# One time line for all tiles, one activation table set, and one-hot columns kept by stage

## The chip, the core and the metric

The kernel runs on one core of a Trainium2 chip. The core has five engines that run their own instruction streams in order and wait for each other at semaphores: TensorE (PE, matmuls; PEld is its weight load), VectorE (DVE), ScalarE (ACT), GpSimd (POOL) and SyncE (SP, which here only issues loads). The metric is the device time of one execution in microseconds. The kernel before takes 1128.44 us (median of 3 runs, 1127.2 to 1128.48).

## What is computed

x has 2 batches of 16000 rows with 512 channels, in bf16. The reference, cut to what matters:

```python
z = sum(xp[:, i:i+T, :] * dw_enc[i] for i in range(3))   # depthwise filter over time
z = silu(z)
res, q = z, 0
for s in range(4):                                       # four codebooks of 8 rows
    cb = codebooks[s]
    d2 = sum(res * res) - 2.0 * res @ cb.T + sum(cb * cb)
    idx = d2.argmin(-1)
    q, res = q + cb[idx], res - cb[idx]
y = sum(qp[:, i:i+T, :] * dw_dec[i] for i in range(3))   # second depthwise filter
```

## The kernel before, in words

The rows are cut into 18 tiles of 1792 rows (128 partitions by G = 14 groups), which overlap by two rows. A tile passes through five steps:

- **load**: 14 transposing DMAs on SP (L213) bring x, with the channels on the partitions, into one of two buffers XT (XT0 and XT1, in the trace XT_149 and XT_150). Two POOL copies (L214, L215) fill the halo columns. A load into a buffer waits until the last reader of the tile before in it has run.
- **front**, for each of the four 128-channel parts: three multiplications by a filter tap (the taps, L222) and two additions (L225, L226) on DVE; then SiLU without a division, Exp on ACT (L227), plus one on DVE (L232), Ln and Exp on ACT (L234, L235), and the product on DVE (the gate, L240) into one of three buffers ZB.
- **select**: PE makes the products of each row with itself and with the codebooks (L252, L255), DVE reduces them (L273, L274), and then decides stage 0, 1 and 2 in a chain of small operations (L296 to L311); between two stages a correction by the codebooks' products goes over PE (L318 to L341). A decision ends in a one-hot block OH (L311), which POOL copies (L312) into the tile's array OHA. Then PE transposes OHA in seven windows (L350), and DVE copies them to OHW (L351).
- **resid**: 24 updates subtract the chosen codebook rows from ZB. PE does the matmuls with OHW (L362, L363) into one of three PSUM buffers; three of four updates are written back by ACT (L367), the fourth by DVE (L369). The score of the last codebook (L283, L284), its decision and a second pass of the windows follow.
- **back**: seven decodes, two or three matmuls each (L380 to L384), copied by ACT into Y (L385), and the stores, issued by POOL (L408).

ACT holds one set of function tables at a time; the built program has a table load wherever the next function is not in the set that is held. Exp and Ln come from different sets in the kernel before.

The order in which the code records its steps is made at the end: iteration n takes the steps of front for tile n, select for n-1, resid for n-2 and back for n-3, spreads each list evenly over the iteration, and sorts. A scheduler of the framework then makes the engines' streams from these steps with its own costs; it moves instructions, and it fixes their order on each engine.

Of the kernel before, what the change touches and what calls it, by code (L numbers as in the profile page):

```python
# [17 lines left out]
def kernel(  # L18
# [41 lines left out]

    IDENT = const.tile([P, P], BF16, name="IDENT")
# [12 lines left out]
    WDBC = const.tile([P, K, D], BF16, name="WDBC")  # L74
    CB4 = const.tile([P, D], BF16, name="CB4")
    cbf = codebooks.flatten_outer_dims()
    wd_rows = bass.AP(tensor=dw_dec.tensor, offset=dw_dec.offset, ap=[[0, P], [D, K], [1, D]])
    with nc.allow_non_contiguous_dma(reason="small weights"):
        for k in range(K):
            nc.scalar.dma_start(out=WENC_b[:, :, k], in_=dw_enc[k].rearrange("(i p) -> p i", p=P))  # L80
        for j in range(4):
            nc.scalar.dma_start(out=CB4[NC * j:NC * (j + 1), :], in_=cbf)
        nc.scalar.dma_start(out=WDBC, in_=wd_rows)
# [6 lines left out]
    for i in range(KT):  # L90
        pt = psS.tile([P, 512], F32, name="pt", tag="pss")
        ptb = pt.bitcast(BF16)[:, 0:NC]
        nc.tensor.transpose(ptb, CB4[0:NC, i * P:(i + 1) * P], IDENT[0:NC, 0:NC])
        nc.vector.tensor_copy(CBT[:, i, :], ptb)
        nc.vector.tensor_scalar(out=CBM2[:, i, :], in0=ptb, scalar1=-2.0, scalar2=None, op0=ALU.mult)
# [65 lines left out]


    WDEC = []
    for v, taps in enumerate(((0, 1, 2, None), (None, 0, 1, 2), (None, None, 0, None), (None, 2, None, None))):
        w = const.tile([P, D], BF16, name=f"WDEC{v}")
        nc.gpsimd.memset(w, 0.0)
        for j, tap in enumerate(taps):
            if tap is not None:
                nc.vector.tensor_tensor(out=w[NC * j:NC * (j + 1), :], in0=CB4[NC * j:NC * (j + 1), :],
                                        in1=WDBC[NC * j:NC * (j + 1), tap, :], op=ALU.mult)  # L170
# [3 lines left out]
    for s in range(3):  # L174
        SM = const.tile([P, 1], F32, name=f"SM{s}")
        nc.vector.tensor_reduce(out=SM, in_=IDENT.rearrange("p (j s c) -> p j s c", s=Nq, c=C)[:, :, s, :], axis=AX.XY, op=ALU.add)
        nc.vector.tensor_scalar(out=SM, in0=SM, scalar1=-1.0, scalar2=None, op0=ALU.mult)
        for u in range(2):
            w = const.tile([P, D], BF16, name=f"CBN{s}_{u}")
            nc.gpsimd.memset(w, 0.0)  # L180
            j = 1 + u
            nc.vector.tensor_scalar(out=w[NC * j:NC * (j + 1), :], in0=CB4[NC * j:NC * (j + 1), :],
                                    scalar1=SM[NC * j:NC * (j + 1), :], scalar2=None, op0=ALU.mult)
# [4 lines left out]
    OHA = [const.tile([P, G + 2, NC], BF16, name=f"OHA{b}") for b in range(NOH)]  # L188
# [97 lines left out]
    def decide(st, s):  # L286
# [23 lines left out]
        OH = small.tile([P, G, C], BF16, name="OH")  # L310
        nc.vector.tensor_tensor(out=OH, in0=KY, in1=M.to_broadcast([P, G, C]), op=ALU.is_equal)  # L311
        nc.gpsimd.tensor_copy(OHA[st["n"] % NOH][:, 1:G + 1, cs], OH)  # L312
# [32 lines left out]
    def windows(st):  # L345
# [3 lines left out]
        for k in range(GH):  # L349
            nc.tensor.transpose(pwb[:, k * P:(k + 1) * P], A[:, 2 * k:2 * k + 4, :].rearrange("p g c -> p (g c)"), IDENT)  # L350
        nc.vector.tensor_copy(W[:, :, PADC:PADC + P], pwb[:, 0:GH * P].rearrange("p (k c) -> p k c", c=P))  # L351
# [68 lines left out]
    def select(st):  # L420
# [6 lines left out]
        yield lambda: windows(st)  # L427

    def resid(st):
# [9 lines left out]
        yield lambda: windows(st)  # L439
# [4 lines left out]

    NT = len(tiles)
    load(tiles[0])
    for n in range(NT + 3):
        if n + 1 < NT:
            load(tiles[n + 1])
        steps = []  # L450
        for off, gen in ((0, front), (1, select), (2, resid), (3, back)):
            if 0 <= n - off < NT:
                w = list(gen(tiles[n - off]))
                steps += [((j + 0.5) / len(w), off, f) for j, f in enumerate(w)]
        for _, _, f in sorted(steps, key=lambda t: t[:2]):
            f()
# [30 lines left out]
```

## Time and profile before

| | |
|---|---|
| runs | 1128.48, 1127.2, 1128.44 us |
| profiled execution | 1130.45 us, span of its instructions 1128.6 us |
| mean granted TensorE clock | 0.843 |
| ACT busy | 919.7 us (81%) |
| DVE busy | 768.0 us (68%) |
| PE busy | 667.1 us (59%) |
| POOL busy | 103.2 us (9%) |
| table loads on ACT | 137, 1283 ns each |
| loads of a tile | 18, each of 14 DMAs, 18.2 to 23.2 us to issue |

The share of an engine is its busy time over the span. A row of a timeline gives start and duration in microseconds; a row of a group gives the busy time, the mean of one in nanoseconds, and the idle time of the engine just before it. "A <- B" names what ended a wait. PEclk is the clock that TensorE was granted, as a share of its full speed. Names carry a buffer number (ZB_122, P_3209); P is the scratch of one channel part in front.

### The profile page before, as it was taken

What the parts mean: (1) busy time and instruction counts of PE and PEld (TensorE: products, weight loads), DVE (VectorE), ACT (ScalarE), POOL (GpSimd) and SP (SyncE); (2) the same over time, 40 slices, a digit from 0 to 9 for tenths busy, and PEclk for the clock granted to TensorE, in tenths of its full rate; (3) what the DMA queues carried; (4) which work ended last, traced back from release to release, by engine and by line L of the source; (5) the groups of instructions that cost most, each with busy time, mean ns of one, the idle gap of its engine ahead of it and who ended that gap; (6) DMA issues with size and microseconds to landing.
All of it is one profiled execution on the core that took longest, in us unless ns stands there. A gap on an engine that the chain in (4) does not pass through costs nothing.

```text
span 1128.6 us, 12123 instructions
## 1 busy us (share of the span) xinstructions
PE 667.1 (59%) x4459; PEld 372.7 (33%) x4459; DVE 768.0 (68%) x1520; ACT 919.7 (81%) x803; POOL 103.2 (9%) x219
## 2 busy tenths in 40 slices
PE   0035577473664828474756647575648364759983
PEld 0023244232342414232333324242424232335542
DVE  7897787777566575858666666868675759456631
ACT  0796999999968798887979797989897897956672
POOL 4100101100010100001010100000100100011001
PEclk9987898797886969687887979798969696979996
DMA  5222302314032040504131221414130602020113
GB/s 112 63 63 43 66 9 58 102 29 112 19 77 54 22 109 1 129 1 106 26 89 43 75 57 55 73 50 82 45 86 2 130 1 65 1 66 9 58 65 127
DMA packets 142907, 67.13 MB, mean 59 GB/s; under 512 B 139852, under 2 KB 140460, under 8 KB 140588
## 3 DMA queue, kind: packets, MB, share of 16 engines
q1 hardware_dynamic: 137088, 33.06, 15.1%
q0 software_dynamic: 3840, 32.77, 9.3%
q10 hardware_dynamic: 1920, 0.53, 0.2%
q8 instruction: 35, 0.57, 0.2%
q14 instruction: 24, 0.20, 0.1%
HBM read 0.53 MB, written 32.77 MB: 30 GB/s over the span
## 4 chain that ended last, share of the span: by engine, by line
ACT 45%; SPq 17%; DVE 14%; PE 14%; issue 5%; DMA 3%; POOL 1%; ACTq 0%; POOLq 0%; DVEq 0%
SPq L213 17%; ACT ZB_124 L367 5%; ACT ZB_122 L367 5%; ACT ZB_123 L367 5%; ACT Y L385 5%; ACT LN L234 5%; ACT L235 5%; PE pgr L255 4%; ACT L234 4%; PE pu L363 3%; PE pu L362 3%; DMA XT_150<-in_x_dram 1%; DMA XT_149<-in_x_dram 1%; DVE rr L273 1%; PE pgr L252 1%
## 5 line engine op out<-in xcount | busy, mean ns | idle before, releaser
L385 ACT CAST Y<-py 128x1024 bf16<-128x1024 f32 x126 | 128.1, 1023 | 75.4 <-PE py L384 57.6
L367 ACT CAST ZB_122<-pu 128x896 bf16<-128x896 f32 x108 | 94.0, 907 | 23.3 <-PE pu L363 22.5
L362 PEld LDWEIGHTS <-IDENT 128*128 128x128 bf16 x648 | 69.1, 107 | 124.8 <-DVE S L274 42.2
L362 PE MATMUL pu<-ZB_122,IDENT 128*128 128x512 bf16 (+1 forms) x216 | 85.2, 394 | 29.5 <-DVE S L274 14.8
L367 ACT CAST ZB_123<-pu 128x896 bf16<-128x896 f32 x108 | 93.8, 909 | 10.5 <-PE pu L363 9.6
L362 PE MATMUL pu<-ZB_123,IDENT 128*128 128x512 bf16 x216 | 83.8, 388 | 29.6 <-DVE S L274 12.1
L367 ACT CAST ZB_124<-pu 128x896 bf16<-128x896 f32 x108 | 93.6, 911 | 6.2 <-PE pu L363 5.5
L362 PE MATMUL pu<-ZB_124,IDENT 128*128 128x512 bf16 x216 | 82.9, 384 | 18.7 <-DVE S L274 7.2
L234 ACT ACT_TABLE_LOAD x68 | 87.2, 1283 | 1.2
L255 PE MATMUL pgr<-ZB_122 128*128 128x152 bf16 (+1 forms) x672 | 58.6, 242 | 41.8 <-DVE ZB_122 L240 41.8
L252 PE MATMUL pgr<-MSK,IDENT 128*128 128x456 bf16 (+3 forms) x180 | 64.6, 359 | 21.4 <-ACT Y L385 9.7
L369 DVE TENSOR_TENSOR ZB_124<-ZB_124,pu 128x896 bf16<-128x896 bf16 x36 | 39.1, 1086 | 50.4 <-PE pu L363 50.4
L369 DVE TENSOR_TENSOR ZB_122<-ZB_122,pu 128x896 bf16<-128x896 bf16 x36 | 39.1, 1086 | 48.9 <-PE pu L363 48.9
L255 PEld LDWEIGHTS <-ZB_122 128*128 128x128 bf16 x672 | 52.0, 106 | 56.8 <-DVE ZB_122 L240 43.8
L235 ACT ACT_TABLE_LOAD x54 | 69.3, 1283 | 1.0
L369 DVE TENSOR_TENSOR ZB_123<-ZB_123,pu 128x896 bf16<-128x896 bf16 x36 | 39.1, 1086 | 37.0 <-PE pu L363 37.0
L408 POOL DMA_DIRECT2D out_dram<-Y x66 | 40.2, 613 | 243.5 <-ACT Y L385 243.5
L255 PE MATMUL pgr<-ZB_123 128*128 128x152 bf16 (+1 forms) x672 | 57.4, 238 | 5.1 <-DVE ZB_123 L240 4.9
L255 PEld LDWEIGHTS <-ZB_123 128*128 128x128 bf16 x672 | 50.8, 104 | 24.3 <-issue 12.8
L273 DVE TENSOR_REDUCE rr<-pgr 128x6 f32<-128x768 f32 (+1 forms) x54 | 41.8, 775 | 19.7 <-PE pgr L255 19.3
L255 PE MATMUL pgr<-ZB_124 128*128 128x152 bf16 (+1 forms) x672 | 53.1, 228 | 0.8 <-DVE ZB_124 L240 0.4
L380 PE MATMUL py<-WDEC_211,OHW_259 128*128 128x512 bf16 x35 | 15.7, 449 | 60.8 <-DVE OHW_259 L351 52.5
(1268 smaller groups left out, 1853.7 us busy)
## 6 DMA issues: line engine op xcount, KB each, us to landing
out_dram<-Y POOLq DMA_DIRECT2D x18, 1568.0 KB, 8.4
out_dram<-Y POOLq DMA_DIRECT2D x14, 196.0 KB, 8.1
XT_149<-in_x_dram SPq DMA_TRANSPOSE x126, 2.8
XT_150<-in_x_dram SPq DMA_TRANSPOSE x126, 2.8
out_dram<-Y POOLq DMA_DIRECT2D x30, 12.0 KB, 2.0
out_dram<-Y POOLq DMA_DIRECT2D x2, 210.0 KB, 8.1
WDBC<-in_dw_dec_dram ACTq DMA_DIRECT2D x1, 384.0 KB, 4.4
out_dram<-Y POOLq DMA_DIRECT2D x2, 126.0 KB, 7.8
```

The source lines that it names most:

```text
L213: nc.sync.dma_start_transpose(out=X[:, :, g + 1, :], in_=src[g])
L234: nc.scalar.activation(LN, pk[1], ACT.Ln)
L235: nc.scalar.activation(pk[1], LN, ACT.Exp, scale=-1.0)
L252: nc.tensor.matmul(o, lhsT=IDENT, rhs=MSK[:, 0:nb, c0:c1], start=True, stop=False)
L255: nc.tensor.matmul(o[:, u * w:(u + 1) * w], lhsT=Z[:, i, b0 + u, N3:N3 + P], rhs=Z[:, i, b0 + u, c0:c1], start=False, stop=(u == nb - 1 an ...
L273: nc.vector.tensor_reduce(out=grp(st["rr"], g0, g1)[:, :, :, 0], in_=v[:, :, :, N3:N3 + P], axis=AX.X, op=ALU.max)
L362: nc.tensor.matmul(o, lhsT=IDENT, rhs=zg[:, k0:k0 + nk, :], start=True, stop=False)
L363: nc.tensor.matmul(o, lhsT=CBN[s, u][:, i * P:(i + 1) * P], rhs=W[:, k0:k0 + nk, PADC:PADC + P], start=not on_act, stop=True)
L367: nc.scalar.copy(zg, v)
L369: nc.vector.tensor_tensor(out=zg, in0=zg, in1=v, op=ALU.add)
L385: nc.scalar.copy(Y[:, 2 * k:2 * k + 2, :].rearrange("p g d -> p (g d)"), py)
L408: nc.gpsimd.dma_start(out=view[p0:p1, lo:hi, :], in_=Y[p0:p1, lo:hi, :])
```

## The change

The change has four parts.

1. Before anything else one table set is asked for that has both Exp and Ln.
2. The steps of all tiles go on one time line. Tile n is loaded at n-1; front takes n to n+1, select n+1.05 to n+1.6, resid n+1.6 to n+2.6, back n+2.6 to n+3.4. All steps are sorted by these times once, instead of iteration by iteration.
3. OHA has the stage ahead of the group, so that a decision writes its one-hot block there itself and POOL's copy goes. A window is then 32 columns of one stage; the transposes are made per stage, 21 after the third decision and 7 after the fourth, where there were 7 and 7, and the two copies to OHW take 96 and 32 partitions, where both took 128.
4. The constants follow the new layout: CB4 is loaded by 16 DMAs of 8 rows and CB1 by one, in place of four of 32 rows, and WDEC and CBN are made with masks JM.

```diff
+    nc.scalar.preload_act_table_set("natural_log_exp_and_others")
...
-        for j in range(4):
-            nc.scalar.dma_start(out=CB4[NC * j:NC * (j + 1), :], in_=cbf)
+        nc.scalar.dma_start(out=CB1, in_=codebooks.flatten_outer_dims())
+        for s in range(Nq):
+            for j in range(4):
+                nc.scalar.dma_start(out=CB4[NC * s + C * j:NC * s + C * (j + 1), :], in_=codebooks[s])
         nc.scalar.dma_start(out=WDBC, in_=wd_rows)
...
-    OHA = [const.tile([P, G + 2, NC], BF16, name=f"OHA{b}") for b in range(NOH)]
+    OHA = [const.tile([P, Nq, G + 2, C], BF16, name=f"OHA{b}") for b in range(NOH)]
...
-        OH = small.tile([P, G, C], BF16, name="OH")
+        OH = OHA[st["n"] % NOH][:, s, 1:G + 1, :]
         nc.vector.tensor_tensor(out=OH, in0=KY, in1=M.to_broadcast([P, G, C]), op=ALU.is_equal)
-        nc.gpsimd.tensor_copy(OHA[st["n"] % NOH][:, 1:G + 1, cs], OH)
...
-    def windows(st):
+    def windows(st, s0, s1):
...
         for k in range(GH):
-            nc.tensor.transpose(pwb[:, k * P:(k + 1) * P], A[:, 2 * k:2 * k + 4, :].rearrange("p g c -> p (g c)"), IDENT)
-        nc.vector.tensor_copy(W[:, :, PADC:PADC + P], pwb[:, 0:GH * P].rearrange("p (k c) -> p k c", c=P))
+            for s in range(s0, s1):
+                nc.tensor.transpose(pwb[NC * s:NC * (s + 1), k * P:(k + 1) * P],
+                                    A[:, s, 2 * k:2 * k + 4, :].rearrange("p g c -> p (g c)"), IDENT)
+        r = slice(NC * s0, NC * s1)
+        nc.vector.tensor_copy(W[r, :, PADC:PADC + P], pwb[r, 0:GH * P].rearrange("p (k c) -> p k c", c=P))
...
-        yield lambda: windows(st)
+        yield lambda: windows(st, 0, 3)
...
-    load(tiles[0])
-    for n in range(NT + 3):
-        if n + 1 < NT:
-            load(tiles[n + 1])
-        steps = []
-        for off, gen in ((0, front), (1, select), (2, resid), (3, back)):
-            if 0 <= n - off < NT:
-                w = list(gen(tiles[n - off]))
-                steps += [((j + 0.5) / len(w), off, f) for j, f in enumerate(w)]
-        for _, _, f in sorted(steps, key=lambda t: t[:2]):
-            f()
+    order = []
+    for n, st in enumerate(tiles):
+        order.append((n - 1.0, 0, lambda st=st: load(st)))
+        for off, dur, gen in ((0.0, 1.0, front), (1.05, 0.55, select), (1.6, 1.0, resid), (2.6, 0.8, back)):
+            w = list(gen(st))
+            order += [(n + off + dur * (j + 0.5) / len(w), off, f) for j, f in enumerate(w)]
+    for _, _, f in sorted(order, key=lambda t: t[:2]):
+        f()
```

How this moves instructions, at three places of the steady part. A tap is a TENSOR_SCALAR whose input is XT0 or XT1; before, its line is L222, in the changed kernel L237.

On DVE before, the last two taps of a tile in XT1 are these (P0_3207 and P1_3209):

```order
L304 TENSOR_TENSOR V_2934<-PR3_2843,rr3_2844 128x112
L222 TENSOR_SCALAR P0_3207<-XT1_150,WENC_102 128x1792
L307 TENSOR_TENSOR KEY1_263<-V_2934,CCB_170 128x112
L222 TENSOR_SCALAR P1_3209<-XT1_150,WENC_102 128x1792
L309 TENSOR_REDUCE M_2937<-KEY1_263 128x14
L225 TENSOR_TENSOR P0_3207<-P0_3207,P1_3209 128x1792
```

The next tile in XT1 is first read 29 rows after P1_3209, by P2_3934:

```order
L226 TENSOR_TENSOR P0_3594<-P0_3594,P2_3598 128x1792
L369 TENSOR_TENSOR ZB2_124<-ZB2_124,pu_3032 128x7x128
L222 TENSOR_SCALAR P2_3689<-XT0_149,WENC_102 128x1792
L222 TENSOR_SCALAR P2_3934<-XT1_150,WENC_102 128x1792
L222 TENSOR_SCALAR P2_3996<-XT1_150,WENC_102 128x1792
L232 TENSOR_SCALAR P1_3596<-P1_3596 128x1792
```

So before, 29 of the 80 rows that a tile has on DVE lie between the two; for tiles 3 and 4 it is 69 and 48. On DVE now, the last taps in XT1 are P0_3442 and P1_3444:

```order
L237 TENSOR_SCALAR P0_3442<-XT1_165,WENC_117 128x1792
L316 TENSOR_TENSOR PR_3260<-S_3137,CCF_184 128x112
L237 TENSOR_SCALAR P1_3444<-XT1_165,WENC_117 128x1792
L319 TENSOR_TENSOR V_3262<-PR_3260,TR_3258 128x112
L386 TENSOR_TENSOR ZB2_139<-ZB2_139,pu_3268 128x7x128
L322 TENSOR_TENSOR KEY0_288<-V_3262,CCB_185 128x112
```

The next tile in XT1 is first read by P2_4094:

```order
L241 TENSOR_TENSOR P0_3756<-P0_3756,P2_3760 128x1792
L237 TENSOR_SCALAR P2_3930<-XT0_164,WENC_117 128x1792
L237 TENSOR_SCALAR P2_4094<-XT1_165,WENC_117 128x1792
L247 TENSOR_SCALAR P1_3664<-P1_3664 128x1792
L237 TENSOR_SCALAR P2_4150<-XT1_165,WENC_117 128x1792
L288 TENSOR_REDUCE rr_3622<-pgr_3623 128x6
```

Now 66 rows lie between them, and so for every tile from the third on.

On ACT before, the last update of one tile (ZB1) and the first of the next (ZB2) are almost neighbours, and Exp and Ln with their table loads follow:

```order
L385 CAST Y_2542<-py_2916 128x1024
L367 CAST ZB2_124<-pu_2968 128x7x128
L367 CAST ZB2_124<-pu_2983 128x7x128
L227 ACTIVATE P1_3209<-P0_3207 128x1792
L234 ACT_TABLE_LOAD
L234 ACTIVATE LN_3300<-P1_3209 128x1792
L235 ACT_TABLE_LOAD
L235 ACTIVATE P1_3209<-LN_3300 128x1792
L227 ACTIVATE P1_3454<-P0_3452 128x1792
```

On ACT now, five Exp and Ln stand between the last update cast of ZB1 and the first of ZB2, without a load:

```order
L384 CAST ZB1_138<-pu_2835 128x7x128
L242 ACTIVATE P1_2960<-P0_2958 128x1792
L249 ACTIVATE LN_3012<-P1_2790 128x1792
L250 ACTIVATE P1_2790<-LN_3012 128x1792
L249 ACTIVATE LN_3055<-P1_2960 128x1792
L250 ACTIVATE P1_2960<-LN_3055 128x1792
L384 CAST ZB2_139<-pu_3005 128x7x128
```

The whole ACT stream has one table load now, at its start, where there were 137.

More of the change, by code (lines that the diff above doesn't have):

```diff
@@ L75 @@
     CB4 = const.tile([P, D], BF16, name="CB4")
-    cbf = codebooks.flatten_outer_dims()
+    CB1 = const.tile([NC, D], BF16, name="CB1")
     wd_rows = bass.AP(tensor=dw_dec.tensor, offset=dw_dec.offset, ap=[[0, P], [D, K], [1, D]])
@@ L92 @@
         ptb = pt.bitcast(BF16)[:, 0:NC]
-        nc.tensor.transpose(ptb, CB4[0:NC, i * P:(i + 1) * P], IDENT[0:NC, 0:NC])
+        nc.tensor.transpose(ptb, CB1[:, i * P:(i + 1) * P], IDENT[0:NC, 0:NC])
         nc.vector.tensor_copy(CBT[:, i, :], ptb)
@@ L438, in resid @@
         yield lambda: decide(st, 3)
[L439 removed]
+        yield lambda: windows(st, 3, 4)
     def back(st):
```

32 lines of the change are left out of this document (20 added, 12 removed).

## The prediction

> **What bounds the kernel now.** I read the share of each engine first, then the chain that ended last, then one period of the loop.
>
> ```profile
> PE 667.1 (59%) x4459; PEld 372.7 (33%) x4459; DVE 768.0 (68%) x1520; ACT 919.7 (81%) x803; POOL 103.2 (9%) x219
> ```
>
> ScalarE (ACT) is the busiest: 919.7 us of 1128.6. Its table loads are three groups:
>
> ```profile
> L234 ACT ACT_TABLE_LOAD x68 | 87.2, 1283 | 1.2
> L235 ACT ACT_TABLE_LOAD x54 | 69.3, 1283 | 1.0
> L227 ACT ACT_TABLE_LOAD x15 | 19.2, 1283 | 7.6 <-DMA CB_93<-in_codebooks_dram 7.4
> ```
>
> That is 137 loads, 175.7 us. But ACT is idle for 19% of the span, and the chain of waits names a second bound:
>
> ```profile
> ACT 45%; SPq 17%; DVE 14%; PE 14%; issue 5%; DMA 3%; POOL 1%; ACTq 0%; POOLq 0%; DVEq 0%
> ```
>
> SPq is the queue that issues the 14 transposing DMAs of a tile (L213). Its timeline has one row per tile; the distance of two rows is the period:
>
> ```profile
> 116.39 19.07 SPq L213 DMA_TRANSPOSE XT_149<-in_x_dram  x14
> ...
> 455.85 22.80 SPq L213 DMA_TRANSPOSE XT_149<-in_x_dram  x14
> 518.88 23.08 SPq L213 DMA_TRANSPOSE XT_150<-in_x_dram  x14
> ```
>
> Two such periods as windows, cut at rows of that queue (busy us of PE, PEld, DVE, ACT, POOL, then the granted clock):
>
> ```profile
> 214.39:262.91 48.52, 35.36 (x214) 18.91 (x215) 38.98 (x77) 48.12 (x42) 3.89 (x6) 0.87 0.17 39
> 455.85:518.88 63.03, 37.75 (x251) 20.74 (x249) 41.75 (x81) 51.56 (x45) 5.16 (x11) 0.78 0.25 59
> ```
>
> The early period, 48.5 us, is ACT's own: it is busy for 48.1 of it. The later one is 63.0 us with the same work, and ACT idles for 11.5 us. The chain of waits in order of time shows what fills it:
>
> ```profile
> 394.45 0.81 SPq L213
> ...
> 414.25 4.72 DMA XT_150<-in_x_dram
> ...
> 420.30 0.69 DVE P_3934 L222
> ...
> 455.20 0.58 DVE P_3687 L222
> ```
>
> It is a ring. The last tap of a tile frees the buffer XT1; the load of the tile after next is issued and lands; VectorE (DVE) then runs that tile's first tap (P_3934), queued ahead of the scoring of another tile, so everything on DVE waits behind it; 35 us later comes the last tap of the next tile (P_3687), and the other buffer goes the same way from 455.85 on. That the load waits for the last tap, and when that runs:
>
> ```profile
> L222 DVE TENSOR_SCALAR P_3209<-XT_150,WENC x1: 677/677/677, 392.0 to 392.0; 128x1792 bf16<-128x1792 bf16 x1
> ...
> SPq L213 <- DVE P_3209 L222: 40.3, 1, 40.3
> ```
>
> By the order in the section on the change, 29 DVE rows lie before between a buffer's last tap and its next first tap, of 80 in a period. For the early tiles they are 69 and 48, and there the period is ACT's 48.5 us. So the kernel has two bounds: ACT with its table loads (48.5 us per tile), and, for most of the run, the ring through the load (63 us there; the mean over the run is 58.7).
>
> **The change part by part.**
>
> *Table loads.* The new ACT order holds one. In the 63 us period I count 8, 8 x 1.283 = 10.3 us, so ACT needs 51.56 - 10.3 = 41.3 us per tile. Alone this is hidden from the later periods, where ACT waits anyway; it lowers the floor from 48.5 us.
>
> *The order.* The 29 rows become 66 of 80, in every steady period. Load, landing and halo copy take 420.30 - 392.0 = 28 us from the last tap on. At a period of 47 us, 66 rows are 39 us; the load is covered. It comes back into the loop when 66/80 of a period falls under 28 us, at 34 us, below every floor named here. The work that hides it is DVE's own queue; if that cover went, the price is the 12 to 15 us between the two periods.
>
> *What is late next.* Floors per tile are ACT 41.3, DVE 41.75, PE 37.75 at clock 0.78. Nearly equal engines do not pack fully. The new order puts 5 of a tile's 12 Exp and Ln between the last update cast of a tile and the first of the next; at about 1.7 us each (the single row below) that is 8.5 us, and the other 41.3 - 8.5 = 32.8 us of ACT lie among the updates. In the gap runs a chain: last update, score of the residual, decision, one-hot windows, first update matmuls of the next tile. The end of the run, where no taps disturb it, gives its bare length:
>
> ```profile
> 1035.33 1.09 DVE L369 TENSOR_TENSOR ZB_122<-ZB_122,pu 128x896 bf16<-128x896 bf16 x1 [0.45 <-PE pu L363]
> ...
> 1045.53 0.61 DVE L351 COPY OHW_261<-pW 128x896 bf16<-128x896 bf16 x1
> ```
> ```profile
> 427.18 1.70 ACT P_3516 L235
> ```
> ```profile
> L304 DVE TENSOR_TENSOR V<-PR,TR 128x112 bf16<-128x112 bf16 x54 | 15.1, 280 | 1.4
> ```
>
> 10.8 us from 1035.33 to 1046.14. The new DVE order adds in this stretch about 25 small operations of the selection, at most 25 x 0.28 = 7 us, if none falls into a wait for PE. So the chain is 10.8 to 17.8 us; I take the middle, 14.2, since half of those operations stand next to rows that wait for PE. The period is 32.8 + 14.2 = **47.0 us**. Bounds: 41.75 us if the chain hides (DVE full), 52 us if it is 17.8 and the other part runs at 96%, somewhat under the 48.12/48.52 seen.
>
> *One-hot columns.* The POOL copies (L312) go; POOL was idle for 91%, and a copy of about 0.3 us on the way to the windows is saved, which I price at nothing beside the chain's width. PE gets 28 transposes per tile instead of 14:
>
> ```profile
> L350 PE MATMUL pW<-IDENT,OHA_257 x14: 218/219/230, 504.5 to 582.2; 128*128 128x128 bf16 x14
> ```
>
> 14 more are at most 14 x 0.219 = 3.1 us and, pipelined as in the trace, far less; I take 1 us, inside the chain's width. The Trainium skill speaks against this part: "TensorEngine Tiling (Array Packing)", Key Properties, says that a change of the tiling mode drains TensorE, and the new transposes fill 32 columns each. By it the few switches per tile would each expose one latency of 0.219 us, a microsecond or two per tile, about 25 us over the run; no run here shows such a switch, and the sum goes without it.
>
> *Setup.* CB4 takes 16 small DMAs and CB1 one, where there were four (the first 100 us as a window, then the rows):
>
> ```profile
> 0.00:100.00 100.00, 19.08 (x121) 12.76 (x122) 81.63 (x183) 58.00 (x38) 19.71 (x56) 0.89 0.38 79
> ```
> ```profile
> 2.33 4.36 ACTq L82 DMA_DIRECT2D CB_93<-in_codebooks_dram  x4
> 6.73 0.59 ACTq L83 DMA_DIRECT2D WDBC<-in_dw_dec_dram  x1
> ...
> 27.92 0.69 DVE L222 TENSOR_SCALAR P_320<-XT_149,WENC 128x1792 bf16<-128x1792 bf16 x1
> ```
>
> 13 more at up to 4.36/4 = 1.09 us move WDBC's issue to as late as 21 us; the page has 4.4 us from its issue to landing, so 25 us, and in the new DVE order the first taps stand behind operations on WDBC. They began at 27.9 us; with those operations after the wait I allow 0 to 8 us of delay. Against it, ACT loses its table loads there too; what DVE can gain by that is at most its idle time, 100 - 81.6 = 18.4 us, of which some 6 are before any data; I take 10 less 8, so the first 116.4 us become 114.
>
> *End.* Last tap of the last tile, and windows of the last two selections:
>
> ```profile
> 996.18 0.68 DVE L222 TENSOR_SCALAR P_7970<-XT_150,WENC 128x1792 bf16<-128x1792 bf16 x1
> ...
> 1036.57 0.63 DVE L351 COPY OHW_258<-pW 128x896 bf16<-128x896 bf16 x1 [0.15 <-PE pW L350]
> ...
> 1054.67 0.42 DVE L273 TENSOR_REDUCE rr<-pgr 128x2 f32<-128x256 f32 x1
> ...
> 1070.29 0.62 DVE L351 COPY OHW_259<-pW 128x896 bf16<-128x896 bf16 x1 [0.15 <-PE pW L350]
> ```
>
> From 996.2 to the end are 132.4 us. From 1070.3 on (58 us) nothing changes. The 74 us before it hold the updates of two tiles; in the new order the first of them is half done at that tap, and a tile takes 33.7 us there (1070.29 - 1036.57), so about 50 us remain: 108 us.
>
> *Sum.* Before: 116.4 + 15 periods of 58.7 (from 116.4 to 996.2) + 132.4 = 1128.6. After: 114 + 15 x 47.0 + 108 = 927. The profiled execution took 1130.45 us, 2 us over its span and 2 us over the median of the runs; so I predict **930 us**. At 41.75 us per period it is 851, at 52 us 1005.
>
> **The rivals.**
>
> 1. *The chain hides* and DVE or ACT runs full: 41.75 to 43 us, 114 + 15 x 42.5 + 108 = 860. For it: ACT ran at 99% in the early period. Against: three near-equal engines, and the chain has no other tile's updates to cover it. 0.11.
>
> 2. *PE becomes the bound.* While the updates run, PE also has decode and the next score. With 3.1 us of extra transposes and 37.75 us at clock 0.78, plus the 10.8 us in which PE mostly waits for DVE, it needs 51.7 us: 998. Against: in 214 to 263 us the clock was 0.87. The Trainium skill ("TensorE: Matmul & The Clock Gate", Part 1) says that idle windows of about 3.4 us lower the clock and steady work raises it, which would make denser work cheaper; here 0.78 goes with the period with the long stall and 0.87 with the denser one, which agrees. 0.14.
>
> 3. *The load stays in the ring*: if loads take far longer beside denser stores, or a halo copy is late, because one of the two now stands on POOL behind the stores of a tile. Then only the table loads on the ring go, some 3 of 1.283 us: 58.7 - 3.8 = 54.9 us, 1046. Against: 39 us of cover for 28. 0.06.
>
> 4. *Slower than before.* The selection and the residual's score stand one after the other in front of the next tile's updates, with nothing of ACT beside them. Bare, the second is 10.8 us; the first is about 15.6 us in the end of the run (the reduce at 1054.67 to the copy at 1070.29). If both are exposed, with 3.1 us more of transposes, the period is 32.8 + 29.5 = 62.3, 1157. It decides above 60.4 us ((1128.6 - 222)/15). Against: in the new order both end in neighbouring rows. 0.03.
>
> That table loads stay is ruled out by the order.
>
> **How the numbers follow.** The forecast, periods of 44 to 51 us, has 0.66; the rivals have 0.11, 0.14, 0.06 and 0.03. 882 to 987 is the forecast's own range; I widen it to 865 to 995, which takes in most of rival 1 and half of rival 2 and leaves out about 0.18. A difference under 0.2% is what a measurement of this kernel cannot tell from none. Faster: 0.96; same: 0.01; slower: 0.03.
>
> **What would show it.** One table load on ACT. Rows of the load's queue 47 us apart from the fifth tile on, SPq nearly gone from the chain, and no tap waiting for the halo copy. ACT near 41.3 us per period and 85 to 90% busy in it, its remaining idle time in one piece per tile, ended by update matmuls. The forecast is wrong if the periods stay above 55 us, if SPq keeps over 10% of the chain, or if PE has no idle time while ACT waits.

## The result and the profile after

The changed kernel takes 888.68 us (median of 4 runs, 888.19 to 890.07), the kernel before 1128.46 us beside it: a ratio of 0.7871, 95% interval 0.7845 to 0.7896. The forecast was 930 us with a range of 865 to 995. The profiled execution took 890.07 us with a span of 888.2 us.

The page of the changed kernel, the shares of the engines and the chain that ended last:

```profile
PE 631.2 (71%) x4660; PEld 358.7 (40%) x4711; DVE 739.6 (83%) x1526; ACT 736.1 (83%) x667; POOL 79.7 (9%) x143
...
DVE 39%; ACT 29%; PE 22%; issue 5%; SPq 3%; DMA 1%; ACTq 0%; POOL 0%; POOLq 0%; DVEq 0%
```

ACT's busy time falls from 919.7 to 736.1 us, the loads' issue (SPq) from 17% of the chain to 3%. The timeline of the load's queue gives the period again, one row per tile, here the fifth, the tenth, the eleventh and the last but one:

```profile
122.21 19.09 SPq L228 DMA_TRANSPOSE XT_164<-in_x_dram  x14
...
343.97 24.56 SPq L228 DMA_TRANSPOSE XT_165<-in_x_dram  x14
388.33 23.41 SPq L228 DMA_TRANSPOSE XT_164<-in_x_dram  x14
...
654.55 23.06 SPq L228 DMA_TRANSPOSE XT_164<-in_x_dram  x14
```

(654.55 - 122.21) / 12 = 44.36 us, and no two periods in this stretch differ by more than 0.4 us. Before, the mean was 58.7 us and single ones had 63. One period as a window (length, busy us of PE, PEld, DVE, ACT, POOL, then the granted clock), and the last tap of the last tile:

```profile
343.97:388.33 44.36, 35.00 (x260) 19.84 (x262) 39.83 (x81) 40.78 (x38) 4.29 (x6) 0.92 0.40 84
```
```profile
785.33 0.68 DVE L237 TENSOR_SCALAR P_8265<-XT_165,WENC 128x1792 bf16<-128x1792 bf16 x1
```

ACT is busy for 92% of the period, and its idle time is 44.36 - 40.78 = 3.6 us where it was 11.5. By the prediction's three terms:

| term | predicted | measured |
|---|---|---|
| up to the fifth load | 114 | 122.2 |
| 15 periods | 15 x 47.0 = 705 | 663.1, or 15 x 44.2 (to the last tap at 785.3) |
| from the last tap to the end | 108 | 102.9 |
| span | 927 | 888.2 |

### The profile page after: what moved, and what is told of

Read it like the earlier page. It is cut to its first block, busy times and chain, and to the rows that moved or that the text cites. A ratio compares the mean times of both kernels' runs of the same rounds, so it can differ in the third digit from the quotient of the medians.

```text
span 888.2 us, 12372 instructions
## 1 busy us (share of the span) xinstructions
PE 631.2 (71%) x4660; PEld 358.7 (40%) x4711; DVE 739.6 (83%) x1526; ACT 736.1 (83%) x667; POOL 79.7 (9%) x143
## 4 chain that ended last, share of the span: by engine, by line
DVE 39%; ACT 29%; PE 22%; issue 5%; SPq 3%; DMA 1%; ACTq 0%; POOL 0%; POOLq 0%; DVEq 0%
PE pu L380 9%; PE pu L379 7%; ACT ZB_139 L384 6%; ACT ZB_137 L384 5%; ACT Y L402 5%; ACT ZB_138 L384 5%; SPq L228 3%; DVE ZB_137 L255 2%; DVE ZB_138 L255 2%; DVE ZB_139 L255 2%; PE pgr L270 2%; PE py L397 2%; DVE M L324 1%; DVE ZB_138 L386 1%; DVE ZB_139 L386 1%
## 5 line engine op out<-in xcount | busy, mean ns | idle before, releaser
L402 ACT CAST Y<-py 128x1024 bf16<-128x1024 f32 x126 | 130.6, 1043 | 13.8 <-PE py L397 13.8
L384 ACT CAST ZB_138<-pu 128x896 bf16<-128x896 f32 x108 | 95.9, 932 | 18.5 <-PE pu L380 18.0
L384 ACT CAST ZB_139<-pu 128x896 bf16<-128x896 f32 x108 | 95.6, 933 | 17.2 <-PE pu L380 16.7
L384 ACT CAST ZB_137<-pu 128x896 bf16<-128x896 f32 x108 | 95.7, 935 | 10.5 <-PE pu L380 10.5
L379 PEld LDWEIGHTS <-IDENT 128*128 128x128 bf16 x648 | 65.6, 101 | 77.8 <-issue 18.9
L270 PE MATMUL pgr<-ZB_137 128*128 128x152 bf16 (+1 forms) x672 | 56.4, 232 | 50.7 <-DVE ZB_137 L255 47.7
L379 PE MATMUL pu<-ZB_137,IDENT 128*128 128x512 bf16 (+1 forms) x216 | 81.1, 375 | 9.3 <-ACT ZB_137 L384 8.2
L379 PE MATMUL pu<-ZB_138,IDENT 128*128 128x512 bf16 x216 | 80.6, 373 | 7.8 <-ACT ZB_138 L384 6.7
L379 PE MATMUL pu<-ZB_139,IDENT 128*128 128x512 bf16 x216 | 80.1, 371 | 8.3 <-ACT ZB_139 L384 7.0
L267 PE MATMUL pgr<-MSK,IDENT 128*128 128x456 bf16 (+3 forms) x180 | 61.0, 339 | 23.2 <-ACT ZB_137 L384 4.8
L270 PEld LDWEIGHTS <-ZB_137 128*128 128x128 bf16 x672 | 48.4, 101 | 70.3 <-DVE ZB_137 L255 52.3
L425 POOL DMA_DIRECT2D out_dram<-Y x66 | 34.1, 521 | 389.6 <-ACT Y L402 389.3
L270 PE MATMUL pgr<-ZB_139 128*128 128x152 bf16 (+1 forms) x672 | 53.3, 226 | 3.0 <-ACT ZB_139 L384 2.9
L270 PE MATMUL pgr<-ZB_138 128*128 128x152 bf16 (+1 forms) x672 | 53.6, 226 | 2.5 <-ACT ZB_138 L384 2.5
L270 PEld LDWEIGHTS <-ZB_139 128*128 128x128 bf16 x672 | 46.6, 98 | 18.4 <-issue 9.1
L270 PEld LDWEIGHTS <-ZB_138 128*128 128x128 bf16 x672 | 46.6, 98 | 17.7 <-issue 8.9
L386 DVE TENSOR_TENSOR ZB_137<-ZB_137,pu 128x896 bf16<-128x896 bf16 x36 | 39.0, 1084 | 12.1 <-PE pu L380 11.8
L380 PEld LDWEIGHTS <-CBN_0_262 128*128 128x128 bf16 x144 | 18.9, 131 | 32.6 <-issue 25.3
```

The lines of the kernel that those rows point to most:

```text
L267: nc.tensor.matmul(o, lhsT=IDENT, rhs=MSK[:, 0:nb, c0:c1], start=True, stop=False)
L270: nc.tensor.matmul(o[:, u * w:(u + 1) * w], lhsT=Z[:, i, b0 + u, N3:N3 + P], rhs=Z[:, i, b0 + u, c0:c1], start=False, stop=(u == nb - 1 an ...
L379: nc.tensor.matmul(o, lhsT=IDENT, rhs=zg[:, k0:k0 + nk, :], start=True, stop=False)
L380: nc.tensor.matmul(o, lhsT=CBN[s, u][:, i * P:(i + 1) * P], rhs=W[:, k0:k0 + nk, PADC:PADC + P], start=not on_act, stop=True)
L384: nc.scalar.copy(zg, v)
L386: nc.vector.tensor_tensor(out=zg, in0=zg, in1=v, op=ALU.add)
```

## The experiments

### The three parts of the change, alone and in pairs

The change was taken apart into three: the one table set (T), the time line (L), and the one-hot columns by stage with the setup that they need (O). Each edit against the kernel before, cut to its core:

```diff
T:
+    nc.scalar.preload_act_table_set("natural_log_exp_and_others")
L:
-    for n in range(NT + 3):
...
+    for _, _, f in sorted(order, key=lambda t: t[:2]):
+        f()
O:
-        OH = small.tile([P, G, C], BF16, name="OH")
+        OH = OHA[st["n"] % NOH][:, s, 1:G + 1, :]
...
-        nc.gpsimd.tensor_copy(OHA[st["n"] % NOH][:, 1:G + 1, cs], OH)
```

Only T:

> The kernel before with nothing but the one table set for Exp and Ln: 1 table load instead of 137, and in its instruction order still 29 rows of DVE between a buffer's last tap and its next first tap. Ring theory (the ring through the load sets the pace): some three of the loads lay on the ring, so periods of 58.7 - 3.8 = 54.9 us, and 114 + 15 x 54.9 + 130 = about 1068 us, with SPq still over 10% of the chain. Rival (the table loads are the cost wherever they stand): 1128 - 136 x 1.283 = about 954 us.

Only L:

> The kernel before with nothing but the new time line: 113 table loads, and in its instruction order 29 rows of DVE between last tap and next first tap, as before (18 to 22 in some tiles). Ring theory: the pace stays, 58 to 59 us per period, and only the end is shorter, by up to 25 us: 1100 to 1130 us. Rival (table loads): 24 fewer, 1128 - 31 = 1097 us. As the prediction's text had it (the time line covers the load, ACT with its loads is left): periods of about 49 us, 960 us.

Only O:

> The kernel before with nothing but the one-hot columns by stage (and the setup that they need): no copies on POOL, 141 table loads, and in its instruction order 52 to 55 rows of DVE between last tap and next first tap. Ring theory: 52 rows of a 50 us period are 32 us, more than the 28 us of a load, so the load is covered and ACT with its table loads is the bound, 48.5 to 51.6 us per period: 120 + 15 x 50 + 130 = about 1000 us, ACT busy over 95% in a period. Rival (table loads): as many as before, so 1128 us, within 1%.

T and L, so the changed kernel without O:

> The changed kernel without the one-hot part: one table set and the new time line, POOL's copies and the old setup. 1 table load, and in its instruction order 29 rows of DVE between last tap and next first tap (22 in some tiles). Ring theory: the ring keeps the pace, 53 to 55 us per period, 114 + 15 x 54 + 105 = about 1030 us, SPq over 10% of the chain. As the prediction's text had it (the time line covers the load and the one-hot part costs or saves next to nothing): within 15 us of the changed kernel, 875 to 905 us.

L and O, the changed kernel without T:

> The changed kernel without the one table set: 109 table loads, some 6 per tile, and 83 rows of DVE between last tap and next first tap. Ring theory: the load is covered, ACT with its loads is the bound: 41.3 + 6 x 1.283 = 49 us per period, 122 + 15 x 49 + 103 = about 960 us. Rival (each table load costs its time wherever it stands): 889 + 108 x 1.283 = 1028 us.

T and O, the changed kernel without L:

> The changed kernel with the old order of the steps (iteration by iteration): 1 table load, 52 to 55 rows of DVE between last tap and next first tap. Ring theory: 52 of 80 rows of a 46 us period are 30 us, just over the 28 us of a load: covered or nearly so, 45 to 48 us per period, 122 + 15 x 46 + 125 = about 937 us, of which 20 us are the longer end. As the prediction's text had it (only the time line opens the ring): about 55 us per period, 122 + 825 + 125 = 1072 us.

What was measured, each of the single parts and pairs in one execution. The period is the mean over the stretch from 300 to 620 us of the distance from one update on DVE to the sixth after it (a tile has six there). The last column is the time from the start of a tile's last update on DVE to the start of the copy to OHW that holds the windows of its last decision. It is the same in nearly every tile of a run; where it alternates, both values stand.

| parts | us | period, us | last update to the last decision's windows, us |
|---|---|---|---|
| none (before) | 1130 | 62.4 | 24.9 |
| T | 1041.4 | 58.1 | 24.0 |
| L | 1096.3 | 58.0 | 18.5 |
| O | 1016.0 | 51.1 | 12.1 to 16.6 |
| T, L | 986.8 | 51.6 | 18.5 |
| L, O | 1017.9 | 51.0 | 9.6 |
| T, O | **838.2** | 40.6 | 10.4 to 11.4 |
| T, L, O (the change) | 888.7 | 44.4 | 11.7 |

The ring theory came near for T (1068 expected), for L (1100 to 1130) and for O (about 1000), where the rivals had 954, 1097 and 1128; for L the two can't be told apart. For T and L it was 43 us too slow, and the prediction's own reading (875 to 905) is 82 us too fast. For L and O the rival came nearer: 1017.9 us against 1028 and 960, since ACT with its loads is busy for 48.9 of 50.9 us and the period is not the 49 us that I had set.

Three things follow.

*The parts do not add.* T is worth 89 us alone and 178 us when O is there. O is worth 114 us alone and 203 us when T is there. Together they are worth 292 us, and a sum of the two alone would have been 203.

*O, which was priced at nothing, is one of the two large parts.* Alone it is worth more than T (114 us against 89). Taken out of the finished change it is worth 98 us (986.8 to 888.7) and T 129 us (1017.9 to 888.7).

*The time line costs time once the other two are in.* L gains 34 us alone and 55 us beside T, gains nothing beside O, and costs 50.5 us on top of T and O (838.2 to 888.7). My expectation for the run without it was 937 us; it is the faster kernel.

What bounds each shows in windows of one period. First O alone, then T and O:

```profile
432.80:484.60 51.80, 37.23 (x263) 21.28 (x267) 41.02 (x83) 51.10 (x47) 4.65 (x7) 0.93 0.29 72
```
```profile
321.40:361.70 40.30, 32.79 (x257) 18.64 (x256) 39.73 (x81) 40.30 (x38) 4.02 (x7) 1.00 0.36 92
```

With O alone ACT is busy for 51.1 of 51.8 us, table loads included: ACT is the bound, as forecast for that run. There each load costs its full time: 141 loads become 1, and 1016.0 - 838.2 = 177.8 us are 1.27 us for each of 140, with 1.283 us as the duration of one. With T and O ACT is busy for 40.3 of 40.3 us, DVE for 39.7: nothing is left between them.

In the kernel before, T's 136 loads are worth 1130 - 1041.4 = 88.6 us, 0.65 us each. So the rival by which each load costs its time wherever it stands is right where ACT is the bound, and wrong by half where it is not. O alone also gives the size of ACT's bound with its loads: 51 us per tile, where the prediction had 48.5 from an early period with fewer ACT instructions (42 against 47 in this window).

### Two waits of nearly the same length

Something else than ACT's own work held the kernel before. The prediction named the ring through the load. This run opens it by other means: one buffer instead of three for the scratch P2, so that the first multiplication of the next tile can't stand so early on DVE.

```diff
+    p2pool = ctx.enter_context(tc.tile_pool(name="p2pool", bufs=1))
...
-            t = ppool.tile([P, R], BF16, name=f"P{k}")
+            t = (ppool if k < 2 else p2pool).tile([P, R], BF16, name=f"P{k}")
```

> The kernel before with one change that is not in the diff: the scratch P2 gets one buffer of its own instead of three, so that the first multiplication of the next tile can't be put so early. POOL's copies, 139 table loads and the old order of the steps all stay; in its instruction order 90 rows of DVE lie between last tap and next first tap. Ring theory: the ring is open, ACT with its loads is the bound, about 50 us per period, 116 + 750 + 130 = about 1000 us. Rival (table loads, or POOL's copies, are the cost): 1128 us or more, since a buffer is taken away.

Measured: 1135.9 us, not 1000. Its chain of waits and one of its periods:

```profile
ACT 57%; PE 18%; DVE 15%; issue 5%; SPq 3%; POOL 1%; DMA 0%; ACTq 0%; POOLq 0%; DVEq 0%
```
```profile
360.25:421.20 60.95, 36.37 (x245) 20.47 (x247) 41.92 (x80) 51.50 (x47) 5.15 (x10) 0.84 0.26 61
```

SPq went from 17% to 3%: the ring is open. The period stayed at 61 us, and ACT still idles for 9.4 us of it. So a second wait of about the same length lay beneath the first, and my expectation, which knew only one, was wrong by 136 us. The wait that is named below is there unchanged: PE waits for the windows' copies for 200.0 us in 18 pieces, and from the last update to the last decision's windows it is 24.9 us, as in the kernel before.

To size the two apart, the next run shortens the load instead, on top of T. The order on PE and ACT stays that of t_only; on DVE one tap stands three rows earlier, at one place of the run, and on POOL a few copies change places:

```diff
-        for g in list(range(G)):
+        for g in list(range(G if st["n"] < NX else GH)):
```

> The kernel before with the one table set, as in t_only, but from the third tile on only the first 7 of a tile's 14 transposing DMAs are issued, so that the other half of the tile keeps the rows of an earlier one (the part of the input that is left out changes the output, not the work). The instruction order of every other engine is that of t_only. Two chains of about the same length are left as the cause of its 58.6 us period: (a) the ring through the load: 7 DMAs less are about 9 to 10 us less between last tap and next first tap, so periods of 49 to 50 us and about 1041 - 14 x 9 = 915 us. (b) the chain from a tile's last update over 27 to 33 rows of VectorE to the windows' copy and the next tile's updates: nothing in it gets shorter, periods of 57 to 58.6 us, 1025 to 1041 us, SPq gone from the chain of waits. Between them: (a) until (b) takes over, 53 to 56 us, 960 to 1000 us.

Measured: 989.6 us, period 52.8. The chain of t_only, then that of this run:

```profile
DVE 25%; SPq 23%; ACT 19%; PE 19%; issue 5%; DMA 5%; POOL 2%; ACTq 0%; POOLq 0%; DVEq 0%
```
```profile
DVE 38%; ACT 32%; PE 22%; issue 4%; DMA 1%; POOL 1%; ACTq 0%; DVEq 0%; POOLq 0%; SPq 0%
```

It is the middle case. The load held t_only at 58.1 us; with less of it the period falls by 5.3 us, SPq leaves the chain, and the second wait takes over at 52.8 us, still 12 us over ACT's 41. What that second wait is stands in this run's timelines of DVE and of PE, and in its chain of waits, in order of time:

```profile
387.97 0.27 DVE L312 TENSOR_TENSOR OH<-KEY,M 128x112 bf16<-128x112 f32 x1
...
402.85 0.61 DVE L352 COPY OHW<-pW 128x896 bf16<-128x896 bf16 x1
```
```profile
388.71 0.56 PE L351 MATMUL pW<-IDENT,OHA 128*128 128x128 bf16 x7 [1.10 <-POOL OHA L313]
403.52 0.61 PE L381 MATMUL py<-WDEC,OHW 128*128 128x512 bf16 x1 [14.24 <-DVE OHW L352]
...
404.77 0.63 PE L363 MATMUL pu<-ZB,IDENT 128*128 128x512 bf16 x1
```
```profile
402.92 0.55 DVE OHW L352
403.47 0.05 issue
403.52 0.61 PE py L381
```

The last decision of a tile is through at 388.2 us, its windows are in PSUM at 389.3, and then PE waits 14.24 us for DVE to copy them to OHW. DVE isn't idle: 19 instructions, most of them taps, additions and gates of other tiles, stand in its queue between the decision and the copy. Behind PE's waiting decode stand the next tile's updates, and behind these ACT's; the chain of waits runs over this copy and this decode. The same wait is in the kernel before, in its waits of PE, which the prediction had not read:

```profile
PE py L380 <- DVE OHW_260 L351: 52.8, 4, 16.3
PE py L380 <- DVE OHW_259 L351: 52.5, 5, 14.8
PE py L380 <- DVE OHW_261 L351: 46.5, 4, 15.4
PE py L380 <- DVE OHW_258 L351: 45.9, 5, 14.8
```

The columns are us in total, times, and the longest. Together they are 197.7 us in 18 waits, the largest wait on PE, 11 us per tile.

### Why the one-hot part removes both

O changes the layout, the transposes, and who copies. One run separates the last from the rest: T, and the old copy of the one-hot block on DVE instead of POOL, with everything else of the one-hot part left as before.

```diff
-        nc.gpsimd.tensor_copy(OHA[st["n"] % NOH][:, 1:G + 1, cs], OH)
+        nc.vector.tensor_copy(OHA[st["n"] % NOH][:, 1:G + 1, cs], OH)
```

> The kernel before with the one table set, as in t_only, and the copy of the one-hot block to OHA on VectorE instead of POOL; the layout of OHA, the 14 transposes per tile, the setup and the order of the steps stay those of before. In its instruction order 57 rows of VectorE lie between last tap and next first tap (29 in t_only) and 12 between a tile's last update and the next windows' copy (27 to 33 in t_only). If the copy's place on POOL is what made the scheduler put these rows so: 4 x 0.3 us more of VectorE than in the run with table set and one-hot part (40.5 us), so 41.5 to 43 us per period and 855 to 885 us. If the layout by stage is what counts: as t_only, about 1041 us.

Measured: **820.6 us**, below the expected range and the fastest run of all, with a period of 40.4 us. One period, and DVE around the same place:

```profile
305.50:345.90 40.40, 33.05 (x245) 19.00 (x248) 40.01 (x85) 40.15 (x38) 4.09 (x6) 1.00 0.35 92
```
```profile
375.74 0.26 DVE L312 TENSOR_TENSOR OH<-KEY,M 128x112 bf16<-128x112 f32 x1
375.92 1.07 DVE L226 TENSOR_TENSOR P<-P,P 128x1792 bf16<-128x1792 bf16 x1
376.93 0.17 DVE L313 COPY OHA<-OH 128x112 bf16<-128x112 bf16 x1
377.02 0.94 DVE L274 TENSOR_REDUCE rr<-pgr 128x6 f32<-128x768 f32 x1
377.89 0.61 DVE L352 COPY OHW<-pW 128x896 bf16<-128x896 bf16 x1
```

From the last decision to its windows' copy are now 2.15 us instead of 14.9. The 19 instructions between them are 3, and in the instruction order the 29 rows between a buffer's last tap and its next first tap are 57: both waits fall to one line of code. PE's decodes wait for the windows' copies for 14.8 us in the whole run, where it was 181.0 us with T alone. The copy itself was never slow on POOL, as this line of the kernel before shows (duration in ns, least, median and greatest):

```profile
L312 POOL COPY OHA_257<-OH x3: 283/387/388, 492.2 to 502.5; 128x112 bf16<-128x112 bf16 x3
```

On DVE it takes 174 to 192 ns. The 0.2 us of difference, four times per tile, are not the 18 us per period. With the copy elsewhere the scheduler lays out DVE's queue in another way. Which of its costs leads to that, no run shows; that moving the copy from POOL to DVE is enough, and that the layout by stage is not needed for it, this one shows. Against T and O (838.2 us) it is 17.6 us faster although the 72 copies stand on DVE: the period is 0.2 us shorter, and the halo copy of the fifth tile begins at 107.2 us instead of 120.9, since the old setup is left.

### The start

In the changed kernel the first tap is later by 11.3 us than before (27.92). Its rows on ACT's queue and on DVE:

```profile
8.47 21.63 ACTq L88 DMA_DIRECT2D CB_94<-in_codebooks_dram  x16
31.04 0.39 ACTq L89 DMA_DIRECT2D WDBC<-in_dw_dec_dram  x1
```
```profile
34.87 0.35 DVE L184 TENSOR_SCALAR WJ_235<-WDBC,JM_226 128x512 bf16<-128x512 bf16 x1 [13.77 <-DMA WDBC<-in_dw_dec_dram]
...
39.17 1.03 DVE L237 TENSOR_SCALAR P_346<-XT_164,WENC 128x1792 bf16<-128x1792 bf16 x1
```

16 small DMAs take 21.63 us to issue, WDBC comes behind them, and DVE waits for it for 13.77 us with the taps of the first tile queued behind. So WDBC's DMA was put first:

```diff
         nc.scalar.dma_start(out=CB1, in_=codebooks.flatten_outer_dims())
+        nc.scalar.dma_start(out=WDBC, in_=wd_rows)
         for s in range(Nq):
...
-        nc.scalar.dma_start(out=WDBC, in_=wd_rows)
```

> The changed kernel with one line moved: WDBC's DMA is issued on ACT's queue before the 16 small DMAs of CB4 and not behind them. If the first taps start at 39 us instead of 28 because the VectorE operations ahead of them wait for WDBC, they start 10 us earlier now and the time falls by 8 to 11 us, to 878 to 881 us. If the load of the first tile or another constant is as late anyway, the time stays at 889 us, within 2 us.

Measured: 884.08 us (882.9 to 885.12), ratio to the kernel before 0.7831 (0.7815 to 0.7848), 4.6 us less than the change: neither case. The wait is still there, under another name:

```profile
32.37 0.43 DVE L188 TENSOR_TENSOR WDEC<-CB,WJ 128x512 bf16<-128x512 bf16 x1 [10.75 <-DMA CB<-in_codebooks_dram]
37.89 1.88 DVE L237 TENSOR_SCALAR P<-XT,WENC 128x1792 bf16<-128x1792 bf16 x3
```

Now the product with CB4 waits for the 16 DMAs, and the first tap moves by 1.3 us only. At the halo copy of the fifth tile the run is 5.7 us ahead of the change (119.3 against 125.0); through which of the constants was not followed. In the next run WDEC and CBN, which nothing needs so early, are made an iteration later. It also has the old order, since that was the faster one:

```diff
+        if n == 1:
+            consts()
         steps = []
```

> The changed kernel with the old order of the steps, iteration by iteration, and with WDEC and CBN made one iteration later, when the first taps are through, instead of ahead of them. The first tap has no operation on WDBC or CB4 ahead of it in VectorE's order. If the first taps then start at about 28 us, as in the kernel before, instead of 39 us, the run with the old order and the early setup (838 us) gets 8 to 11 us shorter: 827 to 831 us. If what was saved comes back as VectorE's work in the second iteration: 834 to 838 us.

Measured: 829.05 us (827.78 to 829.98), ratio 0.7328 (0.7299 to 0.7356), in the first case's range; 9 us less than with the old order alone (838.2). The first tap starts before 22 us:

```profile
21.39 1.00 DVE L239 TENSOR_SCALAR P<-XT,WENC 128x1792 bf16<-128x1792 bf16 x1 [7.07 <-POOL XT L231]
```

It is 17.8 us earlier than in the change and 18.1 us earlier than with the old order alone (39.49); 9 of these remain at the end. This kernel and t_copy_on_dve are both faster than the kernel before and the change; for t_copy_on_dve there is a single time.

### What of the time line costs 3.8 us per period

With T and O in, the time line lengthens the period from 40.6 to 44.4 us. My theory was the selection, which it presses into 0.55 of a period that ends just where the updates begin: 35 rows of DVE, 27 of which take under 0.3 us, stand between a tile's last update and the next windows' copy. So resid was moved away from it:

```diff
-        for off, dur, gen in ((0.0, 1.0, front), (1.05, 0.55, select), (1.6, 1.0, resid), (2.6, 0.8, back)):
+        for off, dur, gen in ((0.0, 1.0, front), (1.05, 0.55, select), (2.0, 1.0, resid), (3.0, 0.8, back)):
```

> The changed kernel with two numbers of the time line changed: resid takes n+2.0 to n+3.0 instead of n+1.6 to n+2.6, back n+3.0 to n+3.8; select still ends at n+1.6, so its decisions are over 0.4 of a period before the updates that need them. In its instruction order 16 rows of VectorE, 5 of them small, lie between a tile's last update and the next windows' copy, where the changed kernel has 35, 26 of them small; 58 rows between last tap and next first tap. If the selection's small rows in that chain are what the time line costs, periods go from 44.4 to 40.5 to 41.5 us; the end gets 0.4 of a tile longer, up to 16 us: 889 - 15 x 3.5 + 10 = about 846 us. If the time line costs by something else (its load's time, its back): 885 to 905 us.

Measured: 896.37 us (895.89 to 899.55), ratio 0.7931 (0.7903 to 0.7959). The rows went from 35 to 16 and the period stayed at 44.35 us; the time from the last update to the last decision's windows only went from 11.7 to 10.5 us. So the number of small rows in that chain isn't what the period shows. From PE's timelines, first the change, then this run:

```profile
403.64 0.61 PE L365 MATMUL pW<-IDENT,OHA_283 128*32 128x128 bf16 x11 [2.55 <-DVE OHA_283 L326]
...
407.87 0.63 PE L399 MATMUL py<-WDEC_254,OHW_286 128*128 128x512 bf16 x1 [0.22 <-DVE P_4092 L237]
...
411.30 0.38 PE L397 MATMUL py<-WDEC_234,OHW_286 128*128 128x512 bf16 x1
```
```profile
462.19 0.93 PE L365 MATMUL pW<-IDENT,OHA 128*32 128x128 bf16 x7 [3.40 <-DVE OHA L326]
...
465.50 1.73 PE L270 MATMUL pgr<-ZB 128*128 128x152 bf16 x12
...
467.40 1.34 PE L270 MATMUL pgr<-ZB 128*128 128x152 bf16 x12
468.57 0.38 PE L379 MATMUL pu<-ZB,IDENT 128*128 128x512 bf16 x1
```

In both, PE stands at a window's transpose, with the next tile's updates queued behind it: in the change 2.55 us for the third decision of the selection, in line_gap 3.40 us for the last decision of the tile before, and behind it the next updates stand after 24 matmuls of the next selection's score. With the old order the corresponding row of the run with T and O waits 1.14 us, and the updates begin there before the windows of the tile before's last decision are copied (at 353.27 us):

```profile
349.37 0.38 PE L380 MATMUL pu<-OHW,CBN 128*128 128x512 bf16 x1 [1.14 <-DVE OHW L368]
```

That a wait on PE in front of the updates is what the time line costs fits all three; that the pressed selection puts it there in both is argued, and no run with a longer selection was made. The record of the granted clock fits too. In the change and in line_gap it falls to 0.50 for 6.83 us once per period, beginning in this wait (at 403.2 and 461.4 us), so PE's work there takes about twice as long; with T and O it is 1.00 from 300 to 640 us. How much of the 3.8 us is the wait and how much the slower clock behind it, no run separates.

## Why the prediction was right, and where not

*Table loads.* One is left. ACT needs 40.8 us per tile; 41.3 were forecast. Right, also that they are partly hidden before; only ACT's bound with them was 51 us and not 48.5.

*The order.* This step failed in its cause. The 66 rows were read rightly, and the load is out of the loop, but the step gave them to the new order of the steps. With L alone, or with T and L, the 29 rows stay and the period is 58.0 and 51.6 us. In these runs the rows open when the copy leaves POOL (52 to 55 with T and O), and the time line only adds to them then (66).

*What bounds the kernel now.* Two bounds were named; there were three. PE's wait of 14 us for the windows' copy was missed, since only the chain and the load's queue were followed. The price of losing the load's cover, 12 to 15 us, was read from a difference that both waits make together; shortening the load alone gave 5.3 us. The chain shows one of two waits that run side by side, and opening the one it shows gave nothing (p2_one_buffer). That the forecast was still near has a reason: its period was worked out from the order of the changed kernel, in which both waits are gone, and needed no word on which part removes them. That the second wait, of which it did not know, is gone from that order as well was luck.

*What is late next.* The mechanism is right in the main: ACT full, but for a chain from the last update to the next tile's first. The five Exp and Ln in it, the rows around its end and its idle times, then the chain's two ends on DVE:

```profile
395.71 1.77 ACT L242 ACTIVATE P_3928<-P_3926 128x1792 bf16<-128x1792 bf16 x1
...
402.34 1.70 ACT L249 ACTIVATE LN<-P_3928 128x1792 f32<-128x1792 bf16 x1 [1.54 <-DVE P_3928 L247]
404.07 1.70 ACT L250 ACTIVATE P_3928<-LN 128x1792 bf16<-128x1792 f32 x1
406.62 0.91 ACT L384 CAST ZB_138<-pu 128x896 bf16<-128x896 f32 x1 [0.85 <-PE pu L380]
```
```profile
393.62 1.09 DVE L386 TENSOR_TENSOR ZB_137<-ZB_137,pu 128x896 bf16<-128x896 bf16 x1
...
404.69 0.61 DVE L368 COPY OHW_287<-pW 96x896 bf16<-96x896 bf16 x1
405.33 0.63 DVE L368 COPY OHW_286<-pW 32x896 bf16<-32x896 bf16 x1
```

The five hold 8.6 us, so ACT has 40.78 - 8.6 = 32.2 us outside (32.8 forecast) and 44.36 - 32.2 = 12.2 us are left for the chain. The prediction chose 14.2 between 10.8 and 17.8: this term was 2.0 us too large, 30 of the 42 us by which the periods together differ. From 395.71 to 406.62 are 10.9 us; the rest of the 12.2 is ACT's short waits among the updates. The small operations of the selection that were to lengthen the chain do stand in it (27 of its 35 rows), but they add little: from the last update to the copy of its last decision's windows (OHW_286) are 11.7 us, where the same distance at the end of the run before, 1035.33 to 1045.53, is 10.2. DVE has hardly a pause between the two rows: the small operations fill what had been waits for PE. And the first update of the next tile waits for the windows of that tile's own first three decisions (OHW_287), which the prediction had in its fourth rival alone; the last decision, which its chain followed, comes 0.2 us later (403.50 against 403.32).

Of the signs that were named, one table load, the load nearly gone from the chain and no tap waiting for the halo copy came true. ACT is busy for 92% of the period and not 85 to 90%, and its idle time is not in one piece: it is six, of which the longest, 1.54 us, is ended by DVE's plus one and not by an update's matmuls.

*One-hot columns.* Priced at nothing; this is the term that was furthest off, 78 to 203 us by what else is in (78 beside L alone, 1096.3 to 1017.9). The direct costs were right: the copy is 0.3 us, and the transposes are cheap. PE's line of those of the third decision in one period:

```profile
L365 PE MATMUL pW<-IDENT,OHA_282 x21: 230/314/314, 355.5 to 359.9; 128*32 128x128 bf16 x21
```

A single one lasts 0.314 us, but they overlap: in the row at 403.64 above 11 take 0.61 us together. The drain that the Trainium skill gives for a change of the tiling mode ("TensorEngine Tiling (Array Packing)", Key Properties) is not visible in these rows; no run measured it by itself.

*Setup.* Forecast 0 to 8 us of delay of the first taps, against 10 us gained. Measured are 11.3 us of delay: WDBC's issue comes at 31.0 and not at 21 us. The small DMAs take 21.63/16 = 1.35 us each and not 1.09, which is 4 us of these 10; the other 6 pass before them, since CB4's first is issued at 8.47 us (before at 2.33), behind three DMAs of WENC that take 5.10 us where they took 1.55, and behind CB1's. The term came out 8 us too small.

*End.* 102.9 us for 108. Right.

*The rivals.* PE did not become the bound: it has 35.0 us per period, not 37.75. The granted clock went from 0.78 in a long period to 0.92, and to 1.00 in the run with T and O, where PE waits 1.14 us at the place where it waits 2.55 us in the change. The Trainium skill ("TensorE: Matmul & The Clock Gate", Part 1) says that idle stretches lower the clock and steady work raises it; the trace agrees, down to single rows: after the wait of 2.55 us the decode at 407.87 takes 0.63 us, and one of the same size at 411.30 takes 0.38. The wait here is shorter than the idle window of about 3.4 us that the prediction took from that page, and the clock fell all the same. That the chain hides altogether (42.5 us) did not happen here, but T and O alone reach 40.6: with the time line this rival fails, and not for the reason that was given against it, that three engines so near to each other do not pack fully.

## What to carry to other kernels

Where two waits of nearly the same length run side by side, the chain of waits names one of them: read the waits of every engine, and ask of each what is queued behind it, before a wait is called the bound. An operation of 0.3 us on another engine can cost much more than its own time through the place that a scheduler gives to what follows it (here 18 us per tile), so read the instruction order for each part of a change apart, and not only for the whole. A part that helps alone can cost once the others are in: take the finished change apart and drop what no longer pays.

## What the runs showed of the hardware

- In these kernels a change of the table set costs the load and nothing around it: 1.27 us for each of 140 loads where ACT is the bound, with 1.283 us for a load. The Trainium skill ("ScalarE: Activation LUTs", What ACT_TABLE_LOAD costs) gives 2.66 us with a drain; these runs do not show the drain.
- ACT and DVE can both be kept busy for 98% and more of a period (40.30 and 39.73 of 40.30 us) with PE at 32.8 us and the clock at 1.00. I had taken it that three engines so near to each other do not pack fully.
- The granted clock fell to 0.50 in a PE wait of 2.55 us (the change) and in one of 3.40 us (line_gap), and in both stayed there for 6.83 us although PE had work again; with T and O no wait of PE from 300 to 640 us is longer than 1.14 us, and it stayed at 1.00. In t_half_load, with waits of 14 us, it stayed low for 10.24, 13.65 or 17.07 us: all of these are multiples of 3.413 us. The periods of the change and of line_gap, 44.36 and 44.35 us, are 13 times 3.413 (44.37) as well; whether the period is held to such a multiple, so that a small gain in the chain can't show, no run tests.
- A small DMA of 8 rows took 1.35 us to issue on ACT's queue, 21.63 us for 16, more than the 19.09 us in which SP issued the fifth tile's 14 transposing DMAs.
